# Which key tiles are multiplied in f16, and the order of two weight-norm passes, in an adaLN + MQA + bilinear-GLU kernel

## The chip, the core and the metric

One core of a Trainium2 chip runs the whole program; the inputs are in HBM and the output goes back there. The metric is the device time of one execution in microseconds, as the median of several runs. The kernel before was measured three times: 1635.51 us median, from 1634.47 to 1637.48.

## The reference, cut to what matters

2048 tokens of 512 numbers, 32 query heads of 16 dimensions, one key head and one value head, and a GLU of width 1792 without a nonlinearity. All inputs are float32.

```python
mod = silu(c) @ w_mod                       # six rows of 512: sa, ca, ga, sb, cb, gb
h = layernorm(x) * (1 + ca) + sa
q = h @ wq;  k = h @ wk;  v = h @ wv        # 32 heads of q, one of k, one of v
p = softmax(q @ k.T / 4)                    # 32 x 2048 x 2048
x = x + ga * ((p @ v) @ wo)
h = layernorm(x) * (1 + cb) + sb
x = x + gb * (((h @ w_gate) * (h @ w_up)) @ w_down)
```

## The kernel before

**Units, tiles and turns.** The attention runs in 32 units: 8 strips of 256 queries, and in each strip 4 chunks of 8 heads, so that unit u is chunk u % 4 of strip u // 4. "First" units are those with u % 4 = 0, "second" ones those with u % 4 = 1. A unit walks over 16 key tiles of 128 keys. For a key tile TensorE computes four score tiles of 128 x 512 (`qk_exp`, L684 and L682), ScalarE takes their exponentials (L690), and one tile later TensorE multiplies them with the values (`pv`, L726), four matmuls in four column groups of 32. The work of one key tile is called a turn here; it runs from one burst of PV matmuls (L726) to the next. TensorE's order in a turn is written out by hand in strings (`FEW`, `MANY`): four score tiles, four tiles of the row maxima of a later unit (`max_mm`, L610, reduced by VectorE at L614), and eight half matmuls of "side" work (L519): the query projection at first, then for each strip the output projection `wo`, gate and up, and down. All engines take their instructions in program order.

**f32 and f16 key tiles.** An ordinary key tile keeps its exponentials in f32 and its PV product runs in f32. For the key tiles listed in `F16_AT` (one tuple for each u % 4), from unit `F16_FROM` on, the exponentials go to one of two sets of buffers (`p_sets`), GpSimd splits them into a high and a low f16 half (`p_split`, L696 and L697, once for each of the four score tiles, over the four turns that follow), and PV becomes three f16 terms, 12 matmuls. Such a tile's PV is issued where the next f16 tile's would stand (`pv_place`); the first one leaves its turn without PV, the last one stands behind the loop. The f16 halves of the values (`v_split`, L708 and L709) are made once, one tile per odd half turn of unit F16_FROM - 1.

**Norms of the weights.** Weights are scaled and split into f16 halves during the first eight units, as a list of items (`wlist`) from which `side_step` takes one at most in each half turn, with gaps given in half turns. The items load a slice from HBM through SyncE's queue into six staging slots (`stage`, L1026). `norms` squares the slices of `wo` (number 3), gate (0) and up (1) on GpSimd and adds them into an accumulator (`square`, L1033 and L1035); wo and gate share the accumulator `ssqs[0]`, up has `ssqs[1]`. Three items behind the last slice of a matrix, four items `sums` follow, each of which reduces a quarter of its accumulator with eight matmul passes on TensorE (L1045). `row_norms` does the down matrix: an item loads row block j, and squares row block j - ROW_LAG on ScalarE with an accumulated sum (L1080); these items stand between the items that load and split gate and up.

```python
acc = ssqs[m % 3 != 0][:, c]
nc.gpsimd.tensor_tensor(acc if i == 0 else t, t, t, op=OP.mult)
if i:
    nc.gpsimd.tensor_tensor(acc, acc, t, op=OP.add)
```

Row blocks and column slices take the six slots in turn, so that a row block's slot is loaded again by the third row block behind it.

Of the kernel before, what the change touches and what calls it, by code (L numbers as in the profile page):

```python
# [30 lines left out]
WARM = (21, 3, 2, 3)  # L31
SQ_GAP = 2.6
LAG = 2
ROW_LAG = 4
SLOTS = (0, 1, 2, 3, 12, 13)
SUM_GAP = 4.0
SUM_LAG = 3
# [11 lines left out]
M_STEP = 23  # L49
PAIRED = 14  # L50
Q_BURSTS = {26: 3, 27: 3, 28: 3, 29: 3}
F16_FROM = 10
F16_AT = ((0, 5, 10), (0,), (0, 4, 9, 13), (0, 4, 9, 13))
P_SHIFT = float(14 * np.log(2.0))

LOW = -3.0e38
# [12 lines left out]
def adaln_mqa_glu_kernel(ctx: ExitStack, tc: tile.TileContext, x_in, wq_in, wk_in, wv_in, wo_in,  # L69
# [51 lines left out]
    for i in range(8):  # L121
# [3 lines left out]
        if i in (4, 5):  # L125
            u = i - 4
# [259 lines left out]
    nc.gpsimd.memset(tok, 0.0)  # L386
    kts16 = sorted({k for ks in F16_AT for k in ks})
    v16 = consts.tile([128, 2, len(kts16), 32], F16, name="v16")
# [59 lines left out]
    def h_halves(b, ks=range(KC)):  # L448
        cs = slice(b * BT, (b + 1) * BT)
        for k in ks:  # L450
            in_halves(h16[:, 0, k, cs], h16[:, 1, k, cs], hf(b, k),
                      None if b else fwd[:, 0:1], nc.gpsimd)
# [202 lines left out]
    pd = {}  # L655
    f16s = [KT * u + k for u in range(F16_FROM, NU) for k in F16_AT[u % NC]]
    while f16s[-1] + 5 >= KT * NU:
# [48 lines left out]
    def v_split(i):  # L706
        k = kts16[i]
        nc.gpsimd.tensor_scalar(v16[:, 0, i], vst[:, k, :], 1.0, 0.0, op0=OP.mult, op1=OP.add)  # L708
        nc.gpsimd.tensor_tensor(v16[:, 1, i], vst[:, k, :], v16[:, 0, i], op=OP.subtract)  # L709
# [32 lines left out]
    def normalise(u):  # L742
        st = {}

        def load():
            st["c"] = work.tile([128, 16], F32, name="rc")
            nc.sync.dma_start(st["c"], pd[u][16:128:32, :].rearrange("j (q f) -> j q f", f=16))
            oc[u] = work.tile([128, ST], F32, name="oc", tag="oc", bufs=2)
            heads = pd[u].rearrange("(j r) (c n) -> c j r n", r=32, c=2)
            for c in range(2):  # L750
                nc.sync.dma_start(oc[u][64 * c:64 * c + 64, :], heads[c, :, 0:16, :])

        def recip():
            nc.vector.reciprocal(st["c"], st["c"])
            st["d"] = dram.tile([4, BT], F32, name=f"ri{u}")
            nc.sync.dma_start(st["d"].rearrange("j (q f) -> (j q) f", f=16), st["c"])

        def spread():
            st["r"] = work.tile([128, ST], F32, name="rr", tag="ev", bufs=3)
            for c in range(2):  # L760
                nc.sync.dma_start(st["r"][64 * c:64 * c + 64, :],
                                  st["d"][:, None, c * ST:(c + 1) * ST].to_broadcast([4, 16, ST]))

        def mult():
            o = oc[u]
            eng = nc.vector if u == NU - 1 else nc.gpsimd
            eng.tensor_tensor(o, o, st["r"], op=OP.mult)
            h = work.tile([128, 2, ST], F16, name="och", tag="och", bufs=6)
            eng.tensor_scalar(h[:, 0, :], o, 1.0, 0.0, op0=OP.mult, op1=OP.add)
            eng.tensor_tensor(h[:, 1, :], o, h[:, 0, :], op=OP.subtract)  # L770
            och[divmod(u, NC)] = h
        return load, recip, spread, mult
# [201 lines left out]
    def late_weights():  # L974
# [24 lines left out]
        gbb = consts.tile([128, D], F32, name="gbb")  # L999
# [5 lines left out]
        def m4():  # L1005
            nc.sync.dma_start(sbb, st["md"][0:1, :].to_broadcast([128, D]))
            nc.sync.dma_start(cbb, st["md"][1:2, :].to_broadcast([128, D]))
# [5 lines left out]
        items = []  # L1013
# [6 lines left out]
        def stage(n):  # L1020
            if "d" in W:
                t = work.tile([128, D], F32, name="wsl", tag="xl", bufs=3)
            else:
                t = stg[:, SLOTS[taken[0] % len(SLOTS)], :]
                taken[0] += 1
            nc.sync.dma_start(t[:, :sl[n][3]], sl[n][2])  # L1026
            st[n] = t

        def square(n):
            m, (i, c), _, w = sl[n]  # L1030
            t = st[n][:, :w]
# [5 lines that stand above are left out]
        def sums(m, j):  # L1037
            w = (D if m > 1 else GC) // 4

            def f():  # L1040
                p = ps_hold("mx")
                st["p"] = p
                for r in range(4):
                    c = (0 if m > 1 else r * GC) + j * w
                    nc.tensor.matmul(p[32 * r:32 * r + 32, :w], onec, ssqs[m % 3 != 0][:, c:c + w], start=True, stop=True)  # L1045

            def g():
                nc.vector.tensor_reduce(cmq[:, m, j:j + 1], st["p"][:, :w], axis=AX.X, op=OP.max)
                ps_give(st["p"])
            return f, g  # L1050

        def norms(order):
            ns = [n for m in order for n in range(len(sl)) if sl[n][0] == m]
            out = []
            waiting = deque()
            for j in range(len(ns) + LAG):
                q = j - LAG

                def f(j=j, q=q):
                    if j < len(ns):  # L1060
                        stage(ns[j])
                    if q >= 0:
                        square(ns[q])
                out.append((SQ_GAP, nothing, f))
                if waiting and j >= waiting[0][0]:
                    out.append((0,) + sums(*waiting.popleft()[1:]))
                if q >= 0 and (q == len(ns) - 1 or sl[ns[q]][0] != sl[ns[q + 1]][0]):
                    waiting.extend((j + SUM_LAG, sl[ns[q]][0], n) for n in range(4))
            out.append((SUM_GAP, nothing, nothing))
            return out + [(2,) + sums(*w[1:]) for w in waiting]  # L1070

        def row_norms(ns):
            out = []
            for j in range(len(ns) + ROW_LAG):
                def f(j=j):
                    if j < len(ns):
                        stage(ns[j])
                    if j >= ROW_LAG:
                        t, n = st[ns[j - ROW_LAG]], j - ROW_LAG
                        nc.scalar.activation(t, t, AF.Square, accum_out=rown[:, n:n + 1])  # L1080
# [3 lines left out]
        def gcols():  # L1084
            nc.vector.tensor_reduce(cmx[:, 0:4], cmq, axis=AX.X, op=OP.max)
            nc.vector.tensor_reduce(cmx[:, 4:5], modT[1][:, :, 32], axis=AX.X, op=OP.max, apply_absolute_value=True)
            nc.vector.tensor_reduce(cmx[:, 5:6], modT[1][:, :, 0], axis=AX.X, op=OP.max, apply_absolute_value=True)

        def cols(j, g):
            nc.vector.tensor_reduce(gm[:, j:j + 1], g, axis=AX.X, op=OP.max, apply_absolute_value=True)  # L1090
# [50 lines left out]
        def last_inverse():  # L1141
# [1 line left out]
            nc.gpsimd.tensor_scalar(gbb, gbb, sca[:, 2:3], 0.0, op0=OP.mult, op1=OP.add)  # L1143

        spread = [(2, tr, trp), (3, bc, scales), (1, nothing, inverse)]
        items += norms((3, 0, 1)) + [(2, nothing, lambda: (gcols(), m4())), (2, nothing, lambda: cols(0, gbb)),
                                     (2, nothing, lambda: cols(1, gab))] + spread

        def split(n):
# [115 lines left out]
    def side_step(step):  # L1265
        if side and step >= side_next[0] and (step % 2 or side[0][1] is nothing):
            gap, f, post = side.popleft()
            side_next[0] = max(side_next[0], step - 1) + gap
            f()
            if post:  # L1270
                posts.append(post)
# [100 lines left out]
    def hooks(u, i):  # L1372
        step = u * NSTEP + i
        if later_h and i % 2 and i > 4:
            b1, k = later_h.popleft()
            h_halves(b1, (k,))
        if u == F16_FROM - 1 and i % 2 and i // 2 < len(kts16):
            v_split(i // 2)
        side_step(step)
        since = i - out_at[0]  # L1380
        if u > 0 and i >= 3 and since in NORM_AT:
            if since == NORM_AT[0]:
                nrm[:] = normalise(u - 1)
            nrm[NORM_AT.index(since)]()
        if since == NORM_AT[3] + 1 and i > 17 and u > 0 and u % NC == 0:
            sb = u // NC - 1
            left = list(fill)
            fill.clear()
            gu, down = ffn_work(sb)
            early = max(len(left) - LATE_Q, 0) if sb == 0 else int(len(left) > 2)  # L1390
            fill.extend(left[:early])
            fill.extend(([step + (2 if sb == 0 else 1)], w) for w in wo_work(sb))
            fill.extend(left[early:])
            fill.extend((["h2", sb], w) for w in gu + down)
# [14 lines left out]
    u = NU - 1  # L1409
# [67 lines left out]
```

## Time and profile before

| | |
|---|---|
| runs | 1635.51 us median, 1634.47 to 1637.48 |
| profiled execution | 1636.99 us, span 1635.0 us |
| TensorE busy | 1616.5 us (99%) |
| VectorE busy | 1399.8 us (86%) |
| ScalarE busy | 1221.8 us (75%) |
| GpSimd busy | 1036.8 us (63%) |

The span is the time from the first to the last instruction; the execution's time has some 2 us more around it. The engines are PE (TensorE), DVE (VectorE), ACT (ScalarE), POOL (GpSimd), SP (SyncE). TensorE's ends are modelled: it counts as busy nearly throughout, so that what it loses is read from the distance between its bursts and not from its idle time.

### The profile page before, as it was taken

The numbers are of one execution on the slowest core, as the hardware profiler recorded it, in microseconds if no ns is written. First come the engines' busy times: TensorE is split into PE (matmuls) and PEld (weight loads), VectorE is DVE, ScalarE is ACT, GpSimd is POOL, SyncE is SP. The second block draws the span as 40 slices with busy tenths as digits, with TensorE's granted clock in tenths as the row PEclk, the third lists the DMA queues.
The fourth block names the chain that finished last, engine by engine and source line by source line (L and its number), as shares of the span: only waits on it lengthen the run. The fifth ranks groups of instructions, "written<-read, shape, count | busy, mean of one in ns | idle before, by whom it ended". The sixth has DMA issues, their size and how long they took to land.

```text
span 1635.0 us, 41269 instructions
## 1 busy us (share of the span) xinstructions
PE 1616.5 (99%) x15897; PEld 749.0 (46%) x15897; DVE 1399.8 (86%) x2433; ACT 1221.8 (75%) x2432; POOL 1036.8 (63%) x1410
## 2 busy tenths in 40 slices
PE   8999999999999999999999999999999999999999
PEld 4332333355533555335543455434545345444766
DVE  8999999999999999999999999999999999980211
ACT  6687888888777888778877788777877777888300
POOL 6857537875755677648756676655857766567422
PEclk9999999999999999999999999999999999999999
DMA  7213323343221000100011001100001001100100
GB/s 258 98 56 97 94 63 107 103 125 96 64 65 31 18 20 27 38 32 18 15 33 36 23 17 33 32 26 26 20 25 33 24 19 33 32 15 22 34 14 14
DMA packets 78998, 79.17 MB, mean 48 GB/s; under 512 B 30408, under 2 KB 59340, under 8 KB 78800
## 3 DMA queue, kind: packets, MB, share of 16 engines
q1 hardware_dynamic: 77744, 76.46, 15.2%
q8 instruction: 125, 2.05, 0.5%
q14 instruction: 73, 0.60, 0.1%
q10 hardware_dynamic: 1056, 0.07, 0.0%
HBM read 56.04 MB, written 17.05 MB: 45 GB/s over the span
## 4 chain that ended last, share of the span: by engine, by line
PE 94%; ACT 3%; DVE 1%; DMA 1%; issue 1%; POOL 0%; ACTq 0%; SPq 0%; DVEq 0%
PE side L519 42%; PE pv L726 30%; PE mx L610 8%; PE sc L684 8%; PE sc L682 3%; ACT P L690 2%; DVE mpart L614 1%; DMA xbig<-in_A_x_dram 1%; PE part L290 0%; PE mxt L638 0%; PE pk L298 0%; PE sc L610 0%; DMA wkv<-in_A_wv_dram 0%; DMA sst<-qd 0%; DVE rel L619 0%
## 5 line engine op out<-in xcount | busy, mean ns | idle before, releaser
L614 DVE TENSOR_REDUCE mpart<-mx 128x1 f32<-128x512 f32 x2016 | 1272.0, 683 | 83.0 <-PE mx L610 74.9
L690 ACT ACTIVATE P<-sc 128x512 f32<-128x512 f32 x1780 | 959.1, 598 | 218.1 <-PE sc L684 175.0
L610 PE MATMUL mx<-kst,sst 48*128 48x512 f16 x2032 | 629.9, 377 | 2.6 <-ACT P L690 0.9
L684 PE MATMUL sc<-sst,kst 51*128 51x512 f16 x1792 | 598.3, 379 | 0.8 <-ACT P L690 0.3
L519 PE MATMUL side<-h2T,wg 64*128 64x256 f16 (+1 forms) x2396 | 540.5, 271 | 0.2 <-ACT P L690 0.2
L519 PE MATMUL side<-h2T,wu 64*128 64x256 f16 (+1 forms) x2396 | 538.3, 270 | 0.0
L726 PE MATMUL pv<-P,vst 128*32 128x512 f32 x3560 | 474.8, 606 | 0.7
L519 PEld LDWEIGHTS <-wg 64*128 64x128 f16 (+1 forms) x2396 | 226.0, 94 | 216.6 <-ACT P L690 147.9
L697 POOL TENSOR_TENSOR glu<-glu 128x512 f16<-128x512 f32 x268 | 310.7, 1159 | 22.3
L519 PE MATMUL side<-wd,glu 64*128 64x512 f16 (+1 forms) x1172 | 271.7, 378 | 0.5 <-ACT tok L687 0.2
L519 PEld LDWEIGHTS <-wu 64*128 64x128 f16 (+1 forms) x2396 | 226.4, 94 | 40.6 <-issue 4.4
L696 POOL TENSOR_SCALAR glu<-glu 128x512 f16<-128x512 f32 x268 | 166.3, 620 | 98.2 <-ACT glu L690 74.1
L610 PEld LDWEIGHTS <-sst 48*128 48x128 f16 x2064 | 191.1, 94 | 31.3 <-issue 13.8
L684 PEld LDWEIGHTS <-kst 51*128 51x128 f16 x1792 | 162.9, 94 | 63.6 <-issue 51.1
L931 POOL TENSOR_SCALAR glu<-gf 128x256 f16<-128x256 f32 x112 | 46.3, 413 | 228.0 <-DVE gf L930 221.2
L690 ACT ACTIVATE glu<-sc 128x512 f32<-128x512 f32 x268 | 149.2, 596 | 51.5 <-PE sc L684 46.0
L519 PEld LDWEIGHTS <-glu 64*128 64x128 f16 (+1 forms) x1172 | 98.7, 95 | 186.9 <-ACT P L690 67.3
L726 PEld LDWEIGHTS pv<-P,vst 128*32 128x32 f32 x3560 | 70.2, 108 | 141.0 <-issue 131.8
L930 DVE TENSOR_TENSOR gf<-side,g 128x256 f32<-128x256 f32 x112 | 46.5, 416 | 79.5 <-ACT g L928 78.0
L682 PE MATMUL sc<-sst,kst 51*128 51x256 f16 x512 | 96.9, 268 | 0.0
L519 PE MATMUL side<-h,wq 64*128 64x512 f16 (+1 forms) x372 | 95.3, 377 | 0.4 <-ACT P L690 0.4
L928 ACT ACTIVATE g<-side 128x256 f32<-128x256 f32 x112 | 42.3, 379 | 66.1 <-PE side L519 65.7
(248 smaller groups left out, 1149.0 us busy)
## 6 DMA issues: line engine op xcount, KB each, us to landing
pd<-ev SPq DMA_DIRECT2D x32, 256.0 KB
kwb<-in_B_w_gate_dram SPq DMA_DIRECT2D x32, 224.0 KB
kwb<-in_B_w_up_dram SPq DMA_DIRECT2D x32, 224.0 KB
sst<-qd SPq DMA_DIRECT2D x180, 32.0 KB
qd<-q SPq DMA_DIRECT2D x16, 256.0 KB
oc<-pd SPq DMA_DIRECT2D x64, 64.0 KB
rr<-ri SPq DMA_DIRECT2D x64, 64.0 KB
x<-in_A_x_dram SPq DMA_DIRECT2D x14, 256.0 KB
```

What stands on the lines that cost most here:

```text
L519: return nc.tensor.matmul(self.p[:, c * w:(c + 1) * w], left[rows], right[rows], start=start and c == 0, stop=stop and c == len(terms) - 1)
L610: nc.tensor.matmul(m, s[64 * a:64 * a + 48, t // 2, p, t % 2 * 128:(t % 2 + 1) * 128], w[64 * a:64 * a + 48, :], start=(i == 0), stop=(i = ...
L614: nc.vector.tensor_reduce(part, m, axis=AX.X, op=OP.max)
L682: nc.tensor.matmul(t[:, c * ST:(c + 1) * ST], keys, s[64 * a:64 * a + 51, c, p, :], start=True, stop=True)
L684: nc.tensor.matmul(t.rearrange("k (c n) -> k c n", c=2), keys, s[64 * a:64 * a + 51, :, p, :], start=True, stop=True)
L690: ex = nc.scalar.activation(ptl[u, kt, p, a], t, AF.Exp)
L696: nc.gpsimd.tensor_scalar(h[:, j, 0], t[:, j], 1.0, 0.0, op0=OP.mult, op1=OP.add)
L697: nc.gpsimd.tensor_tensor(h[:, j, 1], t[:, j], h[:, j, 0], op=OP.subtract)
L726: nc.tensor.matmul(pvb[u][32 * j:32 * j + 32, :], vt, ps[j], start=start and n == 0, stop=stop and n == len(terms) - 1)
L928: nc.scalar.activation(g, p[:, 0:ST], AF.Copy, scale=2.0 ** -45)
L930: nc.vector.tensor_tensor(gf, p[:, ST:2 * ST], g, op=OP.mult)
L931: nc.gpsimd.tensor_scalar(glu()[:, 0, f, :], gf, 1.0, 0.0, op0=OP.mult, op1=OP.add)
```

## The change

Five edits. From unit 9 on instead of 10, first units have f16 tiles 0, 4, 9, 13 instead of 0, 5, 10, and second units 0, 4 instead of 0; third and fourth units keep theirs. The value halves are made in key tiles 10 to 13 of unit 8, for four tiles, instead of key tiles 0 to 5 of unit 9, for six. The norm pass takes wo, up, gate instead of wo, gate, up. Down's row blocks are squared two items behind their load instead of four.

```diff
-ROW_LAG = 4
+ROW_LAG = 2
...
-F16_FROM = 10
-F16_AT = ((0, 5, 10), (0,), (0, 4, 9, 13), (0, 4, 9, 13))
+F16_FROM = 9
+F16_AT = ((0, 4, 9, 13), (0, 4), (0, 4, 9, 13), (0, 4, 9, 13))
...
-        items += norms((3, 0, 1)) + [(2, nothing, lambda: (gcols(), m4())), (2, nothing, lambda: cols(0, gbb)),
+        items += norms((3, 1, 0)) + [(2, nothing, lambda: (gcols(), m4())), (2, nothing, lambda: cols(0, gbb)),
...
-        if u == F16_FROM - 1 and i % 2 and i // 2 < len(kts16):
-            v_split(i // 2)
+        if u == F16_FROM - 1 and i % 2 and 0 <= i // 2 - 10 < len(kts16):
+            v_split(i // 2 - 10)
```

## Rows read from the trace of the kernel before

**Rows 1.** The page's busy times: engine, busy us (share) x instructions.

```profile
PE 1616.5 (99%) x15897; PEld 749.0 (46%) x15897; DVE 1399.8 (86%) x2433; ACT 1221.8 (75%) x2432; POOL 1036.8 (63%) x1410
```

**Rows 2.** Stretches: start:end, length, busy us of PE, PEld, DVE, ACT, POOL; units 24 and 25.

```profile
1158.42:1203.90 45.48, 45.48 (x538) 25.18 (x535) 42.96 (x73) 37.00 (x76) 31.78 (x41) 1.00 0.10 30
1203.90:1250.08 46.18, 46.10 (x490) 21.79 (x486) 44.26 (x77) 36.02 (x71) 29.00 (x41) 1.00 0.12 29
```

**Rows 3.** Stretches: an f16 turn and the f32 turn behind it, unit 14.

```profile
708.01:710.62 2.61, 2.61 (x31) 0.97 (x29) 2.54 (x5) 2.18 (x6) 2.35 (x4) 1.00 0.00 0
710.62:713.45 2.83, 2.83 (x26) 0.87 (x24) 2.52 (x5) 2.59 (x6) 1.56 (x2) 1.00 0.24 90
```

**Rows 4.** Stretches: turns 1 and 5 of unit 17, a second unit.

```profile
843.72:846.57 2.85, 2.77 (x31) 0.95 (x29) 2.78 (x6) 2.41 (x7) 2.68 (x3) 1.00 0.00 0
855.26:858.11 2.85, 2.85 (x34) 1.60 (x34) 2.85 (x6) 2.05 (x5) 0.69 (x1) 1.00 0.00 0
```

**Rows 5.** Groups by line: count, busy us, mean ns of one, idle before.

```profile
L726 PE MATMUL pv<-P,vst 128*32 128x512 f32 x3560 | 474.8, 606 | 0.7
L697 POOL TENSOR_TENSOR glu<-glu 128x512 f16<-128x512 f32 x268 | 310.7, 1159 | 22.3
L696 POOL TENSOR_SCALAR glu<-glu 128x512 f16<-128x512 f32 x268 | 166.3, 620 | 98.2 <-ACT glu L690 74.1 <-PE side L519 8.5 <-PE sc L684 2.1
L726 PE MATMUL pv<-glu,v 128*32 128x512 f16 x804 | 55.7, 382 | 0.0
```

**Rows 6.** Stretches: four turns of unit 1, the column behind POOL is the granted clock.

```profile
115.58:118.41 2.83, 2.79 (x29) 1.01 (x28) 2.80 (x6) 2.11 (x5) 0.00 (x0) 1.00 0.00 0
121.26:126.09 4.83, 3.14 (x31) 0.92 (x29) 2.64 (x6) 2.33 (x6) 4.67 (x6) 0.94 0.52 154
126.09:129.80 3.71, 3.71 (x21) 0.84 (x21) 2.39 (x5) 2.03 (x5) 3.55 (x4) 0.62 0.72 232
129.80:132.30 2.50, 2.50 (x22) 0.76 (x20) 2.39 (x5) 1.94 (x5) 2.42 (x3) 1.00 0.00 1
```

**Rows 7.** Timeline of PE in unit 1: start, length, instruction, [idle before, releaser].

```profile
124.02 0.42 PE L1045 MATMUL mx<-kwb,onec 128*32 128x128 f32 x8 [1.69 <-POOL kwb L1035]
```

**Rows 8.** Timeline of POOL in unit 1.

```profile
111.81 1.13 POOL L1035 TENSOR_TENSOR kwb<-kwb 128x448 f32<-128x448 f32 x1 [4.23 <-PE mx L1045]
...
120.00 0.62 POOL L555 TENSOR_SCALAR q<-qf 128x512 f16<-128x512 f32 x1 [7.06 <-ACT qf L554]
...
122.83 1.13 POOL L1035 TENSOR_TENSOR kwb<-kwb 128x448 f32<-128x448 f32 x1
```

**Rows 9.** Timeline of ACT in units 6 and 7, the squares of down's rows.

```profile
359.94 0.63 ACT L1080 ACTIVATE kwb<-kwb 128x512 f32<-128x512 f32 x1 [0.49 <-DMA kwb<-in_B_w_down_dram]
...
395.81 0.63 ACT L1080 ACTIVATE kwb<-kwb 128x512 f32<-128x512 f32 x1 [0.81 <-DMA kwb<-in_B_w_down_dram]
...
401.10 0.62 ACT L1080 ACTIVATE kwb<-kwb 128x512 f32<-128x512 f32 x1
...
401.71 0.62 ACT L1080 ACTIVATE kwb<-kwb 128x512 f32<-128x512 f32 x1
```

**Rows 10.** Stretches: four turns of units 6 and 7 that hold a square.

```profile
358.41:361.73 3.32, 3.12 (x35) 1.62 (x34) 3.26 (x7) 2.80 (x8) 1.56 (x3) 1.00 0.67 216
391.04:393.96 2.92, 2.92 (x35) 1.52 (x33) 2.61 (x6) 2.80 (x7) 1.52 (x2) 1.00 0.43 121
393.96:397.59 3.63, 3.12 (x35) 1.61 (x34) 3.57 (x8) 2.79 (x8) 1.79 (x4) 1.00 0.23 77
400.43:403.75 3.32, 3.16 (x35) 1.53 (x33) 3.06 (x6) 3.32 (x9) 0.00 (x0) 1.00 0.06 10
```

**Rows 11.** Timeline of POOL at the end of unit 8.

```profile
471.20 1.16 POOL L1170 TENSOR_TENSOR wd<-wsl,wd 128x512 f16<-128x512 f32 x1
...
472.63 0.25 POOL L709 TENSOR_TENSOR v<-vst,v 128x32 f16<-128x32 f32 x1
```

**Rows 12.** Timeline of PE in unit 8, first use of down's last row block.

```profile
474.71 0.38 PE L519 MATMUL side<-wd,glu 64*128 64x512 f16 x1
```

## The prediction, made before the changed kernel was run

> **What bounds the kernel now.** I read four views in this order: the page's busy times, the distance between PV bursts turn by turn, the waits inside the turns that stand out, and the busy times by unit. The page has TensorE busy for 1616.5 of 1635.0 us [rows 1]; the reader is to see that such a number can't say which turn is long, so the distances decide. In the steady part they repeat: a turn with an f32 burst takes 2.83 us, one with an f16 burst 2.61 [rows 3]. In both TensorE is busy to the end, VectorE for 2.54 and 2.52 us. So TensorE's stream of instructions sets the turn, and VectorE stands 0.3 us behind it in an f32 turn, but only 0.07 us behind in an f16 turn. By unit the same shows: TensorE is full, VectorE has 43 of 45.5 us in a first unit and 44.3 of 46.2 in a second one, GpSimd 32 and 29 [rows 2]. The turns that stand out are in unit 1, where two take 4.83 and 3.71 us [rows 6], and in units 6 and 7, where some take 3.3 to 3.6 us [rows 10].
>
> **More f16 tiles.** The list before gives 4 + 4 tiles in units 10 and 11 and 5 x 12 in units 12 to 31, less tile 13 of unit 31, which the code drops: 67 (GpSimd's 268 splits are 4 x 67 [rows 5]). The new list gives 2 in unit 9, 8 in units 10 and 11, 5 x 14 later, less the same one: 79. So 12 f32 bursts become f16 ones. By the groups a burst costs 474.8 / 445 = 1.07 us in f32 (3560 / 8 = 445 tiles) and 55.7 / 67 = 0.83 in f16, 0.24 less [rows 5]; the turns differ by 0.22 [rows 3]. I take 0.23. Each new tile also brings four splits of 0.62 + 1.16 us, 7.1 us of GpSimd [rows 5], 85 us over the 12. In a first unit GpSimd goes from 31.8 to 38.9 of 45.5 us, in a second one from 29.0 to 36.1 of 46.2 [rows 2]. TensorE hides this as long as the last split of a tile is done when its PV comes: it is issued in the middle of the turn of the next f16 tile, and PV stands at the end of the turn behind that, 1.5 x 2.83 = 4.2 us later, of which the split itself needs 1.8.
>
> Seven of the 12 lie in first units or in unit 9's wake, where VectorE has 2.5 us to spare in a unit [rows 2]: 7 x 0.23 = 1.6 us. Five lie in turn 5 of units 13 to 29 (second ones), and there VectorE is busy for all 2.85 us, with the residual and its statistics beside the maxima [rows 4]. A shorter burst can't help in a turn that VectorE fills; turn 1 of such a unit shows it, since it holds an f16 burst and takes 2.85 us all the same [rows 4]. But the lag is worked off later in the unit, so some comes back. The bounds are 0 and 0.23; I take half, 5 x 0.12 = 0.6. Together 2.2 us, between 1.6 and 2.8. Moving the value halves puts four pairs of instructions of 0.25 us each at most [rows 11] into GpSimd's queue at the end of unit 8, among the last splits of down's weights. The last row block there is written at 471.20 + 1.16 = 472.36 [rows 11] and TensorE first needs it at 474.71 [rows 12]: 2.35 us of cover. All four pairs ahead of it take 2.0, and the shorter list of items (below) starts the row blocks earlier; I cost it at nothing. Without that cover it costs up to those 2.0 us, once.
>
> **Up ahead of gate.** Gate's first squares are written into the accumulator that holds wo's, before wo's last `sums` has read it. So in unit 1 TensorE has to wait with an L1045 until GpSimd has done a piece of gate: it starts at 124.02 [rows 7], when GpSimd's L1035 ends at 122.83 + 1.13 = 123.96 [rows 8]. GpSimd was late for two reasons in order: its own addition waited 4.23 us for an earlier L1045, and then its queue stood 7.06 us before L555, the split of a query projection, which waits for ScalarE [rows 8]. Gate's pieces were queued behind. With up in the second place nothing of this is left: up has an accumulator of its own, wo's is last written many microseconds before, and gate comes into it 16 items later. What goes: that turn takes 4.83 us, and a turn with an L1045 that waits for nothing 2.83 [rows 6], so 2.0 us. The turn behind it takes 3.71 instead of 2.50, at a mean granted clock of 0.62 [rows 6]: TensorE's clock fell to 1.2 GHz behind the pause, and the PV burst and what follows it ran at half speed. That is 1.2 us more. Together 3.2 us. Bounds: nothing, if the wait goes elsewhere, and 3.5, if the first turn came down to 2.50 too. I take 3.2, as both turns have undisturbed neighbours of the same make-up. What is late next in those turns is VectorE, with 2.4 of 2.50 us [rows 6]; it was idle during the stall and has nothing to make up.
>
> The Trainium skill ("TensorE: Matmul & The Clock Gate", section "What's actually happening") says that a gate halves the clock after idleness, and that how much runs slowly differs from run to run of the same kernel. The 0.62 of [rows 6] agrees with the halving; that it differs, one profile can't show. By that rule the 1.2 us may be missing in some runs of before, and the gain would be 2.0 instead of 3.2; it is the third rival below.
>
> **Down's squares two items behind.** With six slots shared by two streams a row block's slot is loaded again three items later, so a square four items behind reads the block that was loaded just one item earlier. Twice that load had not landed: ScalarE waits 0.49 us at 359.94 and 0.81 at 395.81 [rows 9], and the exponentials behind it are late for TensorE. Those turns take 3.32 and 3.63 us, where a turn with a square and no wait takes 2.92 [rows 10]: 0.4 + 0.7. At the end the two squares that are left over come 0.6 us apart in one turn [rows 9], which takes 3.32 us with ScalarE full [rows 10]: 0.4. With two items behind, the data has two items' time instead of one, and the 14 squares and the 14 loads need 16 items, which all stand between the splits; the two left-over ones go. The sum is 1.5. A load's slot now waits for the square of one item before instead of two, and SyncE's queue holds the query loads and the normalisation's DMAs behind it. A row block's load that is late by a whole item would bring a wait like the two above. Bounds: 0.8 us worse (one such wait more) to 1.5 better; I take 1.3. The list also ends two items earlier, so down's own splits start up to 3 us earlier; nothing waits for them [rows 11, 12].
>
> **Sum.** 2.2 + 3.2 + 1.3 = 6.7 us, against the profiled execution's 1636.99: 1630.3. That execution is 1.5 us above the median of the runs shown, 1635.51; from there the sum gives 1628.8. The tail behind the loop stays as it is: the number of turns doesn't change, so the side work left over doesn't either.
>
> **Rivals.**
>
> - VectorE takes over. An f16 turn leaves it 0.07 us [rows 3], and a turn that also multiplies a gate tile or ends a unit has more than that on it. If the whole saving of the f16 tiles is lost to VectorE, only 4.5 us are gained: 1631.0. Against it: 58 of the trace's 66 f16 turns stay under 2.70 us, like the one of [rows 3], and VectorE has 2.5 us spare in a first unit [rows 2]. 0.15.
> - The norm pass keeps its stall: up's or gate's `sums` wait for GpSimd as wo's did. Then 3.2 us are not gained: 1632.0. For it: GpSimd's queue is blocked by L555 for up to 7 us [rows 8]. Against it: gate's own `sums` stand three items behind their last addition in the kernel before too, and in its trace no L1045 but the one of [rows 7] waits for GpSimd. 0.10.
> - The clock doesn't fall in the unprofiled runs of before, so that its 1.2 us can't be won: 1630.0. For it: the median run is 1.5 us under the profiled one. Against it: the pause before it, which one order of instructions makes in every execution [rows 7, 8]. 0.08.
> - Slower: GpSimd comes too late for PV. Between tile 13 and the next unit's tile 0 lie three turns, so two splits fall into one turn, 3.6 us in 2.83. If GpSimd's queue is then more than 4.2 - 1.8 = 2.4 us behind, TensorE waits in a burst. That decides from there on; if each of the 12 new tiles cost one split's 1.8 us, it is 21.4 us, less the 6.7: 1650.2. For it: first units come to 38.9 of 45.5 us. Against it: third and fourth units have the same four places now, and the f16 bursts show no idle time before them, 0.0 us over all [rows 5]. 0.05.
>
> The forecast itself has 0.62, with a range of its own from 1627.7 to 1631.5: the sum's bounds while unit 1's stall goes (2.8 + 3.5 + 1.5 = 7.8 us at best, 1.6 + 3.2 - 0.8 = 4.0 at worst).
>
> **How the numbers follow.** 0.2%, what a measurement of this kernel can tell from no change, is 3.3 us: faster is below 1632.2, slower above 1638.8. The forecast, the first and the third rival lie below 1632.2 but for their edges, the second stands on it: faster 0.85, same 0.10, slower 0.05. The range from 1626.0 to 1633.0 reaches over the first three rivals and leaves out the slow one; its lower end is the best sum less 1.7 us, half the spread of the three runs shown and a little over.
>
> **What would show it.** In the changed kernel unit 1 has no turn above 3 us, TensorE no wait for GpSimd in an L1045, and the granted clock no dip there. No square of down's rows waits for its load, and the turns of units 6 and 7 stay below 3.2. First units shorten by 0.2 us to about 45.25, second ones by 0.1 to 0.2. GpSimd's busy time rises by some 85 us. It would be wrong if PV bursts wait for splits, if second units get longer, or if another turn of units 1 to 4 shows the L1045 wait.

## The result, and the profile after

The changed kernel takes 1640.08 us (median of 11 runs, 1638.94 to 1640.9); the kernel before took 1636.48 beside it (11 runs, 1634.47 to 1638.49). The ratio is 1.0021, 95% interval [1.0013, 1.003]: about 3.4 us slower, where 6.7 us faster was forecast. The profiled spans are 1637.6 and 1635.0 us, 2.6 apart.

The page after, busy times (answers to [rows 1]):

```profile
PE 1615.4 (99%) x15945; PEld 748.8 (46%) x15945; DVE 1400.4 (86%) x2433; ACT 1221.9 (75%) x2444; POOL 1119.9 (68%) x1502
```

GpSimd does 83 us more, as worked out (85). TensorE is busy 1.1 us less in a span that is 2.6 us longer, so it must stand still somewhere. Counted by units (each from its first exponential on ScalarE to that of the next unit, to some 0.03 us), the changed kernel is 5.2 us ahead when unit 13 begins (652.31 against 657.49), 2.8 us behind when unit 14 begins, and gets 0.2 back by the end. One unit loses 8.0 us.

Unit 13, a second unit, before (first fence) and after (second fence). In the second fence the first row is the whole unit, the others three stretches in it: start:end, length, busy us of PE, PEld, DVE, ACT, POOL, then the granted clock.

```profile
657.49:703.87 46.38, 46.23 (x391) 14.35 (x389) 43.27 (x74) 35.22 (x68) 24.77 (x33) 1.00 0.13 34
```

```profile
652.31:706.67 54.36, 48.16 (x395) 14.85 (x393) 43.34 (x74) 35.27 (x68) 34.16 (x44) 0.94 0.11 29
...
668.09:674.41 6.32, 0.40 (x5) 0.10 (x4) 1.37 (x3) 0.79 (x3) 5.93 (x6) 0.77 0.00 0
674.41:679.02 4.61, 4.41 (x26) 1.23 (x25) 1.20 (x2) 1.68 (x3) 4.33 (x5) 0.58 0.29 57
679.02:681.86 2.84, 2.84 (x27) 0.89 (x25) 2.54 (x6) 1.92 (x4) 2.76 (x3) 1.00 0.00 0
```

The first two stretches make one turn, from the burst at 668.09 to the next one at 679.02: 10.93 us instead of some 2.8. In the first the burst has begun and waits, and GpSimd is busy for 5.93 of 6.32 us; in the second the mean granted clock is 0.58, so that TensorE is mostly at 1.2 GHz; the third is a usual turn again. TensorE's timeline after shows which instruction stands: the three f16 PV matmuls of tile 0's first three score tiles run, and the rest of the burst waits for the split of the fourth (idle time and releaser in brackets).

```profile
668.09 0.40 PE L726 MATMUL pv<-glu,v 128*32 128x512 f16 x3
...
674.41 1.04 PE L726 MATMUL pv<-glu,v 128*32 128x512 f16 x8 [5.92 <-POOL glu L696]
...
675.65 0.58 PE L726 MATMUL pv<-glu,v 128*32 128x512 f16 x1 [0.20 <-POOL glu L697]
...
679.02 1.06 PE L726 MATMUL pv<-P,vst 128*32 128x512 f32 x8
```

GpSimd's timeline in the same stretch:

```profile
662.31 0.62 POOL L696 TENSOR_SCALAR glu<-glu 128x512 f16<-128x512 f32 x1
663.02 1.16 POOL L697 TENSOR_TENSOR glu<-glu 128x512 f16<-128x512 f32 x1
665.07 0.22 POOL L220 TENSOR_SCALAR rv<-st 128x1 f32<-128x1 f32 x1 [0.90 <-DVE st L822]
...
667.04 2.10 POOL L831 TENSOR_SCALAR n<-x,st,ry 128x512 f32<-128x512 f32 x1
...
672.62 1.15 POOL L841 TENSOR_TENSOR n<-n,n 128x512 f16<-128x512 f32 x1
673.74 0.62 POOL L696 TENSOR_SCALAR glu<-glu 128x512 f16<-128x512 f32 x1
674.44 1.16 POOL L697 TENSOR_TENSOR glu<-glu 128x512 f16<-128x512 f32 x1
```

The third split ends at 664.18. The fourth starts 9.6 us later, and waits for nothing but its turn: the second half of the statistics (L220 to L225) and a layernorm (L831 to L841, 6.7 us) stand ahead of it in GpSimd's queue.

The two edits of the weight norms did what was forecast. Unit 1 takes 41.38 us instead of 44.69, and the turns that answer to the second and third of [rows 6] have lost the wait and the clock's dip:

```profile
121.44:124.16 2.72, 2.72 (x30) 1.01 (x28) 2.43 (x5) 2.12 (x6) 2.64 (x4) 1.00 0.60 179
124.16:126.66 2.50, 2.50 (x21) 0.83 (x20) 2.48 (x5) 2.12 (x6) 2.42 (x3) 1.00 0.51 138
```

Turns of units 6 and 7 with a square, after (against [rows 10]), and squares that answer to [rows 9]; none of the 14 waits now.

```profile
355.28:358.12 2.84, 2.84 (x34) 1.60 (x33) 2.78 (x6) 2.81 (x8) 1.08 (x3) 1.00 0.87 284
387.41:390.33 2.92, 2.92 (x35) 1.52 (x33) 2.61 (x6) 2.80 (x7) 1.52 (x2) 1.00 0.63 190
396.02:398.94 2.92, 2.92 (x36) 1.58 (x34) 2.83 (x7) 2.88 (x7) 0.00 (x0) 1.00 0.08 19
```

```profile
356.20 0.63 ACT L1080 ACTIVATE kwb<-kwb 128x512 f32<-128x512 f32 x1
...
391.26 0.63 ACT L1080 ACTIVATE kwb<-kwb 128x512 f32<-128x512 f32 x1
...
396.69 0.62 ACT L1080 ACTIVATE kwb<-kwb 128x512 f32<-128x512 f32 x1
```

Units 24 and 25, after (against [rows 2]): the first unit is 0.20 us shorter, the second one 0.32 longer. The 0.32 is not the tile's: with the same f16 tiles unit 25 takes 46.2 us in the runs e2, e5, e8 and e10 below, and 46.95 in e1.

```profile
1160.36:1205.64 45.28, 45.28 (x543) 25.25 (x540) 43.03 (x73) 37.02 (x77) 36.48 (x47) 1.00 0.10 30
1205.64:1252.14 46.50, 46.41 (x494) 21.83 (x492) 44.31 (x77) 36.20 (x71) 38.35 (x52) 1.00 0.14 29
```

### The profile page after: what moved, and what is told of

Read it like the earlier page. It is cut to its first block, busy times and chain, and to the rows that moved or that the text cites. A ratio compares the mean times of both kernels' runs of the same rounds, so it can differ in the third digit from the quotient of the medians.

```text
span 1637.6 us, 41530 instructions
## 1 busy us (share of the span) xinstructions
PE 1615.4 (99%) x15945; PEld 748.8 (46%) x15945; DVE 1400.4 (86%) x2433; ACT 1221.9 (75%) x2444; POOL 1119.9 (68%) x1502
## 4 chain that ended last, share of the span: by engine, by line
PE 93%; DVE 2%; ACT 2%; DMA 1%; POOL 1%; issue 1%; ACTq 0%; SPq 0%; POOLq 0%; DVEq 0%
PE side L519 42%; PE pv L726 29%; PE mx L610 9%; PE sc L684 8%; PE sc L682 3%; DVE mpart L614 2%; ACT P L690 1%; DMA xbig<-in_A_x_dram 1%; PE part L290 0%; PE mxt L638 0%; PE pk L298 0%; PE sc L610 0%; DMA wkv<-in_A_wv_dram 0%; DMA sst<-qd 0%; DVE rel L619 0%
## 5 line engine op out<-in xcount | busy, mean ns | idle before, releaser
L690 ACT ACTIVATE P<-sc 128x512 f32<-128x512 f32 x1732 | 935.1, 598 | 210.5 <-PE sc L684 172.3
L726 PE MATMUL pv<-P,vst 128*32 128x512 f32 x3464 | 461.1, 605 | 0.7
L697 POOL TENSOR_TENSOR glu<-glu 128x512 f16<-128x512 f32 x316 | 366.3, 1159 | 26.3
L696 POOL TENSOR_SCALAR glu<-glu 128x512 f16<-128x512 f32 x316 | 196.1, 621 | 102.0 <-ACT glu L690 70.7
L690 ACT ACTIVATE glu<-sc 128x512 f32<-128x512 f32 x316 | 176.2, 596 | 62.0 <-PE sc L684 55.2
```

Source lines behind the costliest of these rows:

```text
L690: ex = nc.scalar.activation(ptl[u, kt, p, a], t, AF.Exp)
L696: nc.gpsimd.tensor_scalar(h[:, j, 0], t[:, j], 1.0, 0.0, op0=OP.mult, op1=OP.add)
L697: nc.gpsimd.tensor_tensor(h[:, j, 1], t[:, j], h[:, j, 0], op=OP.subtract)
L726: nc.tensor.matmul(pvb[u][32 * j:32 * j + 32, :], vt, ps[j], start=start and n == 0, stop=stop and n == len(terms) - 1)
```

## Experiments

The theory (Q, the queue): with tile 4 in a second unit's list, PV of tile 0 comes in turn 5 instead of in the next unit; only in unit 13 does tile 0's fourth split stand behind the layernorm in GpSimd's queue, and the rest of the change gains what was forecast. The rivals stand in the expectations.

**e1: the changed kernel without that one f16 tile.**

```
f16s = [KT * u + k for u in range(F16_FROM, NU) for k in F16_AT[u % NC] if (u, k) != (13, 4)]
```

> The changed kernel, without one f16 tile: key tile 4 of unit 13 is f32 again, so that tile 0's PV comes only in unit 14. Theory Q (the loss is one place: in unit 13 the fourth split of tile 0 stands in GpSimd's queue behind a layernorm chain, PV waits for it 6 us and the clock halves): unit 13 goes from 54.4 back to about 46.4 us, the kernel to 1632 us, 4.5 us or 0.27% faster than before. Rival V (the loss is spread: VectorE and GpSimd are too full for 12 more tiles everywhere): only one tile's share comes back, 1639 to 1640 us.

1633.14 us against 1637.83; ratio 0.9973 [0.9962, 0.9983]. Unit 13 takes 46.24 us, and the only PV wait that is left is one of 0.44 in unit 29. One of 79 tiles turns a slower kernel into a faster one: 0.48% between the two ratios, 7.8 us.

**e2: the changed kernel, that one split a turn earlier.**

```
f16_split.setdefault(min(v + j + 1, n - (j == 2 or v == 13 * KT)), []).append((v, j))
```

> The changed kernel with all its f16 tiles; only the fourth split of unit 13's tile 0 is issued one turn earlier, ahead of the layernorm chain in GpSimd's queue. Theory Q (the order of GpSimd's queue): no wait of PV for a split in unit 13, 46.5 us for the unit, 1632 us, as in the run without the tile, to 0.5 us. Rival G (GpSimd has too much work in unit 13, in whatever order): the wait moves or shrinks, unit 13 stays above 49 us, the kernel above 1634.5.

1634.96; 0.9985 [0.9976, 0.9994]: better than the changed kernel, but short of what Q expected. The PV wait is gone: the fourth split ends at 667.78, just ahead of the second statistics (667.87). Yet unit 13 still takes 51.40 us, with a new stop in turn 12. TensorE in e2:

```profile
691.46 1.01 PE L610 MATMUL mx<-kst,sst 48*128 48x512 f16 x2 [2.42 <-DMA sst<-qd]
...
692.83 1.93 PE L726 MATMUL pv<-P,vst 128*32 128x512 f32 x8
```

SyncE's queue in e2, which issues these transfers:

```profile
687.11 1.27 SPq L864 DMA_TRANSPOSE h2T<-n  x1
688.48 2.87 SPq L575 DMA_DIRECT2D sst<-qd  x6
```

The loads of the next unit's queries stand behind the transpose of the second layernorm half, whose last GpSimd instruction (L841) runs from 685.92 to 687.08; tile 4's splits had delayed it (it ends 33.1 us into the unit, in e1 30.1). So the same extra GpSimd work has a second price in unit 13, through another queue. The turn with the stop takes 6.25 us, and TensorE stays at 1.2 GHz for most of the next, which takes 5.17 at a mean granted clock of 0.53 (the column behind POOL):

```profile
686.58:692.83 6.25, 3.83 (x25) 0.94 (x23) 3.46 (x7) 2.36 (x5) 5.76 (x8) 0.85 0.35 73
692.83:698.00 5.17, 5.17 (x26) 1.25 (x25) 2.12 (x5) 2.28 (x4) 0.00 (x0) 0.53 0.00 0
```

The profiled execution is not a typical one: it took 1637.86 us at a mean granted clock of 0.995. One other of the eleven took 1638.21, and the nine that are left 1633.68 to 1635.83, at 0.997 or 0.998. By the medians e2 is 1.8 us above e1, where unit 13 is 5.2 us longer in the profiles; how long the stop is in the nine, no trace shows. With unit 13 above 49 us and the kernel above 1634.5, e2 stands where rival G put it; e8 decides between the order of the queues and the amount of work.

**e3: no tile 4 in any second unit.** `F16_AT`'s second tuple is `(0,)`.

> The changed kernel with one f16 tile (0) in second units again, for all five of them and unit 9; first units keep four. Theory Q alone, with each tile 4 worth 0.12 us: 1632 us plus 0.5. Theory Q+ (tile 4 of a second unit gives nothing even where it does not stall, since VectorE sets those turns, and its split makes PV wait 0.4 us in unit 29): 1631.0 to 1631.5, at or below the run that drops only unit 13's. Rival V: 1637 or more.

1632.53; 0.997 [0.9959, 0.9981], with six f16 tiles fewer than the changed kernel. This and e1 can't be told apart by their intervals, so e3 doesn't decide whether a tile 4 that doesn't stall is worth anything.

**e4: the kernel before and that one f16 tile.**

```
f16s = sorted([...as before...] + [13 * KT + 4])
```

> The kernel before with a single addition: key tile 4 of unit 13 is an f16 tile too. Theory Q: this one tile makes PV wait in unit 13 as in the changed kernel and costs 7 to 8 us, 1644 us. Rival G (the wait needs the fuller GpSimd of the changed first unit 12): no wait, the kernel within 0.5 us of before.

1647.98 against 1637.83; 1.0063 [1.0049, 1.0077]: 10 us for one tile, more than expected. Unit 13 takes 55.44 us, 9.1 more than before. The PV wait is the same, 5.90 us, but the clock stays low longer. The two turns behind the wait in e4:

```profile
680.38:685.66 5.28, 5.09 (x25) 1.34 (x25) 1.84 (x3) 1.68 (x3) 4.99 (x6) 0.50 0.26 50
685.66:688.94 3.28, 3.28 (x26) 0.93 (x24) 1.91 (x5) 1.92 (x4) 3.12 (x3) 0.85 0.00 0
```

**e5, e6, e7: one part of the change at a time, on the kernel before.** The f16 lists with the value halves; `norms((3, 1, 0))`; `ROW_LAG = 2`.

> The kernel before with the f16 lists, F16_FROM = 9 and the moved value halves alone. Theory Q: first units gain 0.2 us each, some 1.5 us in all, and unit 13 loses 8 us and more (the run with tile 4 of unit 13 alone lost 10): 6 to 8 us slower than before, 1.004 to 1.005. Rival (the two weight edits did the harm): no slower than before.

> The kernel before with up's squares ahead of gate's alone. The forecast's step: no L1045 waits for GpSimd in unit 1, 2.0 us less, and 1.2 more where the clock had fallen: 2.0 to 3.2 us faster, 0.9980 to 0.9988. A profile of the run before it (tile 4 of unit 13 alone) had the wait and no fall of the clock, so the lower end is the likelier. Rival (the wait moves to another sums): same as before.

> The kernel before with down's rows squared two items behind alone. The forecast's step: no square waits for its load, units 6 and 7 shorter by 0.7 and 1.0 us: 1.3 to 1.7 us faster, 0.9990 to 0.9992. Rival (the loads are late for other reasons, and wait in SyncE's queue for squares): within 0.3 us of before.

Against 1637.37: lists 1644.03, 1.0043 [1.003, 1.0055]; up first 1635.2, 0.9986 [0.9977, 0.9995]; lag 1635.21, 0.9986 [0.9978, 0.9995]. In us +7.0, -2.3 and -2.3, together +2.4, where the whole change has +3.4; the intervals reach 2.0 us to either side of the first and some 1.4 of the others, so that the two sums agree within them. The lists alone have unit 13 at 54.20, up first alone unit 1 at 41.37, the lag alone units 6 and 7 at 46.17 and 46.96, all as in the whole change.

**e8 to e11: the query loads earlier,** to part e2's second wait from the first. The same edit goes into e2 (e8), e3 (e9), the changed kernel (e10) and the kernel before (e11):

```
-        if 0 < u < NU - 1 and i == QPRE:
+        if 0 < u < NU - 1 and i == (16 if u >= 12 else QPRE):
```

> The run with unit 13's early split, and from unit 12 on the query loads of a unit are issued eight slots (four turns) earlier, so that SyncE's queue has them ahead of the second transpose, which waits for GpSimd's second layernorm chain. Theory S (that run's 2.4 us wait of TensorE for sst in turn 12 of unit 13, and its clock, came from the order in SyncE's queue): no wait for sst<-qd in any second unit, unit 13 at 46.2 to 46.5 us, some 5 us less there and 0.5 in units 17 and 29: 1630 to 1631, 0.9955 to 0.9965 of before. Rival G (GpSimd has too much work in unit 13): another wait in unit 13, and the kernel stays above 1633.

> One f16 tile in second units, four in first ones, and the query loads four turns earlier from unit 12 on. If a second unit's tile 4 gives about nothing where it does not stall, this is within 0.7 us of the run with the early split and early loads (1630.5, 0.9959): 1630 to 1631. If VectorE leaves room and a tile 4 gives its 0.23, it is 1 us slower than that run, for five tiles.

> The changed kernel with the early query loads alone, the fourth split of unit 13's tile 0 where it was. Theory Q: the wait of PV for the split stays, 6 us and the clock, and unit 13 at 53 to 55 us: 1638 to 1640. Rival (the early loads did all the good in the last run, by freeing SyncE's queue): 1631 or less.

> The kernel before with the early query loads alone. In its profile one turn of unit 21 loses 0.8 us to sst<-qd, in other runs two or three turns of second units lose 0.3 to 1.2. Theory S: these go, 0.5 to 1.5 us faster, 0.9991 to 0.9997. Rival (the reordered normalisation DMAs cost as much): same as before.

e8: 1630.49, 0.9959 [0.9946, 0.9971] against 1637.37. Unit 13 takes 46.0 us at full clock with its tile 4, and SyncE issues the loads ahead of both transposes (e8, the unit, then the queue):

```profile
652.50:698.50 46.00, 45.92 (x395) 14.48 (x391) 43.23 (x74) 35.13 (x69) 34.10 (x44) 1.00 0.15 35
```

```profile
665.91 2.75 SPq L575 DMA_DIRECT2D sst<-qd  x6
675.08 2.11 SPq L864 DMA_TRANSPOSE h2T<-n  x1
...
685.59 1.27 SPq L864 DMA_TRANSPOSE h2T<-n  x1
```

e9: 1630.53, 0.9962 [0.9949, 0.9976] against 1636.93. e10: 1639.38, 1.0016 [1.0007, 1.0025]; the PV wait of 5.9 us is still there, unit 13 takes 54.72: early loads don't touch the first price. e11: 1635.93, 0.9995 [0.9986, 1.0004], no difference that can be told. e8 and e9 are free of both prices in unit 13 and 6.9 and 6.4 us faster than the kernel before. They get there in two ways: keep tile 4 and mend both orders, or leave tile 4 out of second units and load early. That the forecast had 6.7 is chance: the early loads were no part of it, and in the profiles they take some 2 us off units 17, 21 and 25 between e3 and e9.

e8 and e9 differ by tile 4 in the second units alone (and its earlier split in unit 13). By unit (13, 17, 21, 25, 29), e8 has 46.03, 46.04, 46.24, 46.22, 47.05 and e9 46.24, 46.04, 46.24, 46.22, 46.43: tile 4 gives 0.2 us, three times nothing, and costs 0.6, in unit 29, where PV still waits 0.43 us for a split. In e9 no PV waits for one.

## Why the prediction failed

**The step that failed** is the cover of the splits: "TensorE hides this as long as the last split of a tile is done when its PV comes: it is issued in the middle of the turn of the next f16 tile, and PV stands at the end of the turn behind that, 1.5 x 2.83 = 4.2 us later, of which the split itself needs 1.8." That counts the split's own time and nothing that stands ahead of it in GpSimd's queue. In unit 13 that is 6.7 us of layernorm and the statistics before it, so the burst waits 5.92 + 0.20 us, and the lower clock brings the unit to 8.0 more. The Trainium skill ("PSUM — Partial Sum Buffer", section "Engine vs sequencer instructions") calls GpSimd's queue strictly first in, first out; the split that starts at 673.74, behind the layernorm's end, agrees.

**The trace of before showed it, in a unit that the prediction has no rows of.** Five of these instructions in unit 13 before:

```profile
667.47 0.62 POOL L696 TENSOR_SCALAR glu<-glu 128x512 f16<-128x512 f32 x1
...
672.20 2.10 POOL L831 TENSOR_SCALAR n<-x,st,ry 128x512 f32<-128x512 f32 x1
...
677.80 1.16 POOL L841 TENSOR_TENSOR n<-n,n 128x512 f16<-128x512 f32 x1
678.93 0.62 POOL L696 TENSOR_SCALAR glu<-glu 128x512 f16<-128x512 f32 x1
679.63 1.16 POOL L697 TENSOR_TENSOR glu<-glu 128x512 f16<-128x512 f32 x1
```

The burst of turn 5, where the change puts tile 0's PV, stood at 673.25, and the fourth split ended at 680.79: 7.5 us too late for the change's place, and hidden in before because PV came only in the next unit. The prediction took unit 17 for all second units [rows 4]. There the change does hold. GpSimd after, in unit 17, where the f16 burst starts at 857.79:

```profile
854.65 0.23 POOL L220 TENSOR_SCALAR rv<-st 128x1 f32<-128x1 f32 x1 [3.28 <-DVE st L822]
856.60 0.62 POOL L696 TENSOR_SCALAR glu<-glu 128x512 f16<-128x512 f32 x1
857.30 1.16 POOL L697 TENSOR_TENSOR glu<-glu 128x512 f16<-128x512 f32 x1
...
863.43 0.23 POOL L220 TENSOR_SCALAR rv<-st 128x1 f32<-128x1 f32 x1 [1.19 <-DVE st L822]
```

The second statistics come 5.6 us after the burst here and 3.0 us before it in unit 13 (665.07 against 668.09). In unit 17 the fourth split ends at 858.46, just in time for the burst's last matmuls; in unit 29 it is late by 0.44. Counted from the start of the unit, the second statistics stand at 12.8 us in unit 13 and at 21.4 to 21.9 in units 17, 21, 25 and 29; why they come earlier in unit 13 stays open.

**The slow rival** had the mechanism, GpSimd late for PV, but not the place and not the price. It looked at the number of splits in a turn behind tile 13 and set 1.8 us on each of 12 tiles; it was one tile, and another kind of work ahead of the split. Its argument against, that f16 bursts show no idle before them [rows 5], was true of the places that the list had then. The group's row in the changed kernel is:

```profile
L726 PE MATMUL pv<-glu,v 128*32 128x512 f16 x948 | 68.0, 385 | 6.6 <-POOL glu L696 5.9 <-POOL glu L697 0.6
```

**First units, 1.6 us forecast.** Right in kind: 0.20 us in each of five first units and 0.22 in unit 9, 1.2 us together; unit 10 gives 0.15 of it back (45.18 to 45.33). Unit 8 is longer too (45.91 to 46.08), but that comes with down's lag: e7 alone has 46.14, the lists alone (e5) 45.85. VectorE did not take over.

**Second units, 0.6 us forecast.** Next to nothing came: between e8 and e9 0.00 in units 17, 21 and 25 and 0.2 in unit 13, against 0.6 lost in unit 29. The row of turn 1 [rows 4], with VectorE full, was the right one, and the lag that was to be worked off gave nothing. The lower bound, 0, was where the value lay; that a tile could cost time in a second unit had no place in the bounds. Unit 17 of the changed kernel is 0.6 us longer than before (46.62 against 46.04), but not by tile 4: one turn waits for the query loads, here in the loading of TensorE's weights (PEld):

```profile
877.70 0.09 PEld L610 LDWEIGHTS <-sst 48*128 48x128 f16 x1 [0.69 <-DMA sst<-qd]
```

Before has such a turn in unit 21 (47.02 us), e3 without tile 4 in unit 17 (47.26); in e8 to e11, with the early loads, unit 17 takes 46.04 each time.

**Up ahead of gate, 3.2 us forecast.** Unit 1 lost 3.31 us between the two profiles, 2.1 in the turn with the wait (4.83 to 2.72) and 1.2 in the one behind it (3.71 to 2.50), and no L1045 waits for GpSimd: right in place and mechanism. The third rival was partly right too, for the clock. The wait of 1.7 us stands in five profiles that have the old order, but the clock fell in two of them (before and e11), and not in e4, e5 and e7. The two turns that answer to the second and third of [rows 6], in e11 and then in e4:

```profile
121.43:126.23 4.80, 3.12 (x31) 0.92 (x29) 2.62 (x6) 2.31 (x6) 4.64 (x6) 0.95 0.51 144
126.23:130.02 3.79, 3.79 (x21) 0.83 (x20) 2.47 (x5) 2.13 (x5) 3.63 (x4) 0.61 0.73 232
```

```profile
122.95:127.56 4.61, 2.93 (x31) 0.92 (x29) 2.43 (x5) 2.12 (x6) 4.45 (x5) 1.00 0.47 136
127.56:130.06 2.50, 2.50 (x21) 0.83 (x21) 2.48 (x5) 2.12 (x6) 2.42 (x4) 1.00 0.97 305
```

Unit 1 takes 44.7 us with the fall and 43.3 without, against 41.4 with up first, so the edit is worth 3.3 or 1.9 us by the run, and e6's 2.3 over eleven runs, with 1.5 to either side, lies between. The Trainium skill ("TensorE: Matmul & The Clock Gate", section "What's actually happening") says that how much runs slowly differs from run to run of the same kernel. Its example is the start of a kernel; the fall in two of five profiles with the same instructions in unit 1 agrees.

**Down's lag, 1.3 us forecast.** Units 6 and 7 lost 0.68 + 1.00 = 1.7 us in the profiles; e7 has 2.3 us, its interval about 0.8 to 3.6. The forecast waits went and none came, and unit 8 gave 0.2 back. The gain differs by run: in the five profiles with the old lag units 6 and 7 together take 94.06 (e11) to 95.33 us (e4), in those with the new one 93.1.

e3, which is the change without the tiles that failed, is 4.9 us faster than before (3.1 to 6.7), where the forecast without its second units comes to 6.1.

## What to carry to other kernels

When a consumer is moved forward, look up for every instance of it when its last producer ran before the change, in the trace, and not only for one unit of the pattern: 7.5 us of lateness can hide behind a consumer that was late anyway. In an engine that works in order, cover is counted from what stands ahead in its queue, not from the duration of the one instruction; and extra work on it is late for everyone behind, here also for a transpose, and through SyncE's queue for loads that have nothing to do with it. Check where a saving can't arrive (VectorE full, second units) before adding work for it: it leaves the risk without the gain.

## What the runs showed of the hardware

A stop of TensorE can cost more than its wait. The 5.9 us wait lowered the clock in each of the four profiles that have it (after, e4, e5, e10); the same wait made unit 13 longer by 8.0 us in the changed kernel and by 9.1 in e4. The 2.42 us stop of e2 lowered it too in the profiled execution and made the unit some 5 us longer than e1's (51.40 against 46.24); the medians of e2 and e1 are 1.8 us apart, so most executions paid less. The 1.7 us wait of unit 1 lowered it in two of five, and where it did not, the unit is 1.9 us longer, little more than the wait. What stays open is what decides between the two in unit 1, where the order of instructions is the same.
